# A planner that lays out five engines in time: mended durations, port locks and a third raw buffer

## The chip, the cores and the metric

The kernel runs on one core of a Trainium2 chip. Its engines take instructions each from a queue of their own: TensorE (PE, matmuls and transposes), VectorE (DVE), ScalarE (ACT), GpSimd (POOL) and SyncE (SP, which here only issues DMAs). The metric is the time of one execution on the chip in microseconds, the median of several runs.

## What is computed

Attention with four sink columns and a window of 128, in 4 batches of 8 heads over 768 rows of 64 elements, and behind it two matmuls with h cos h between them, for 3072 tokens:

```python
scores = scale * np.matmul(q, k.transpose(0, 1, 3, 2))
keep = is_sink | in_window            # pos < n_sink, or 0 <= row - pos < window
a = softmax(np.where(keep, scores, -1e9))
x = np.matmul(a, v)                   # (4, 8, 768, 64) -> x (3072, 512)
h = x @ w_in                          # (3072, 512) @ (512, 2048)
g = h * np.cos(h)
return (g @ w_out).astype(np.float32) # (3072, 2048) @ (2048, 512)
```

The weights reach the kernel as 64-bit floats, read as pairs of 32-bit integers.

## The kernel before

The 3072 tokens are 12 chunks of 256. A chunk has 8 slots; in a slot 256 of the 2048 columns of h are made (L419), turned into g on ACT and DVE (r L434 and L441, g L452, glo L464), and multiplied with their rows of w_out into two accumulators (acc, L479; in chunk 0, L474). A product of single precision is three matmuls of the parts hi and lo: xhi·lo_in, xhi·hi_in, xlo·hi_in. Chunk 0 multiplies g by w_out in full precision instead.

The weights come in 32 pieces, 16 of w_in and 16 of w_out, 512 KB each as 64-bit numbers. A piece is loaded into one of two raw buffers (`load`, L532), and DVE makes 32-bit numbers of it in three instructions, a shift (L540) and two passes (top L546, low L552). ACT rounds it to the part hi (L579), and POOL or DVE subtracts that to get lo (L582, the remainder). All of this happens in the first 125 us, while the first three chunks' attention runs.

The 24 early heads (`NEH`, those of the first chunk of three batches) load q and k in natural layout (L817), turn them on PE (`pe_turn` L825), copy them out (L409 on DVE, L407 on ACT; names tq, firsts), make scores (s, L850), mask and take the exponential (p, L919 and on ACT), divide (the norm, L953, on POOL, DVE or ACT), turn p on PE (tp, L1025), copy that (firsts), and multiply by v (av, L1077; the input x is split with L354 and the casts xhi and xlo). Later heads have q and k turned by DVE (L807, L879) after loads at L763 and L776, and split scores (s, L906).

All of that, apart from the setup ahead and the last rows behind, is laid out by `Plan.order`: each step was added with the engines it may run on and their durations, what it depends on, and a due time worked out from the constants in `C`. The planner goes through a time of its own. Whenever an engine is free it takes, of the steps whose dependences are done there, the one with the earliest due time, with penalties for POOL (`POOLPEN`) and for other than the first engine (`ALT`). A step that may use the port that POOL and DVE share is marked `port`; of those, one runs at a time. What comes out is a fixed order of instructions on every engine; on the chip each engine goes through its list and waits where a dependence is not there yet. The 160 idle matmuls (`FILL`, L1379) are steps with the latest due time of all, so PE takes one wherever in the planner's time it has nothing else.

## Time and profile before

| what | us |
|---|---|
| median of 3 runs | 741.33 (741.26 to 741.88) |
| the profiled execution | 741.67 |
| its span | 739.9 |
| busy in the span: PE | 722.6 (98%) |
| DVE | 617.0 (83%) |
| ACT | 551.7 (75%) |
| POOL | 195.7 (26%) |
| DMA of raw pieces, 32 of 512 KB, issue to landing | 4.6 and 4.0 each |

A busy time counts from the start of an instruction to its end; matmuls of PE and instructions of DVE overlap at their ends, so a busy engine may start the next one sooner than the mean duration says. Where the text speaks of the spacing that a form holds, it means start to start when the next instruction follows at once.

### The profile page before, as it was taken

The numbers are of one execution on the slowest core, as the hardware profiler recorded it, in microseconds if no ns is written. First come the engines' busy times: TensorE is split into PE (matmuls) and PEld (weight loads), VectorE is DVE, ScalarE is ACT, GpSimd is POOL, SyncE is SP. The second block draws the span as 40 slices with busy tenths as digits, with TensorE's granted clock in tenths as the row PEclk, the third lists the DMA queues.
The fourth block names the chain that finished last, engine by engine and source line by source line (L and its number), as shares of the span: only waits on it lengthen the run. The fifth ranks groups of instructions, "written<-read, shape, count | busy, mean of one in ns | idle before, by whom it ended". The sixth has DMA issues, their size and how long they took to land.

```text
span 739.9 us, 15112 instructions
## 1 busy us (share of the span) xinstructions
PE 722.6 (98%) x4827; PEld 643.5 (87%) x4827; DVE 617.0 (83%) x1679; ACT 551.7 (75%) x1371; POOL 195.7 (26%) x306
## 2 busy tenths in 40 slices
PE   8989999999999999999999999999999999999996
PEld 8777666799999989998979998989999999999995
DVE  6999999768999899999989988987988998875432
ACT  4979777547878878888878798897789789774322
POOL 2201131001434343244334344333112233231000
PEclk9999999999999999999999999999999999999999
DMA  5765655122555465456565342232233332110000
GB/s 150 200 180 163 185 153 185 54 35 41 146 126 115 104 165 139 91 124 150 153 144 142 89 101 50 58 66 43 47 83 56 56 82 53 22 46 2 30 1 32
DMA packets 215896, 71.48 MB, mean 97 GB/s; under 512 B 204288, under 2 KB 204800, under 8 KB 215808
## 3 DMA queue, kind: packets, MB, share of 16 engines
q1 hardware_dynamic: 215232, 70.17, 39.8%
q8 instruction: 40, 0.66, 0.4%
q14 instruction: 48, 0.39, 0.2%
q10 hardware_dynamic: 576, 0.26, 0.1%
HBM read 64.10 MB, written 6.29 MB: 95 GB/s over the span
## 4 chain that ended last, share of the span: by engine, by line
PE 81%; DVE 10%; DMA 3%; ACT 2%; issue 2%; SPq 1%; DVEq 0%; ACTq 0%
PE h L419 32%; PE acc L479 31%; PE av L1101 5%; PE s L906 4%; PE tp L1021 2%; PE acc L474 2%; DMA raw<-in_moe_w_in_dram 1%; PE av L1077 1%; PE idle L1379 1%; DVE w_out L546 1%; DVE p L919 1%; PE s L850 1%; DVE w_in L546 1%; PE tp L1025 1%; DVE w_in L552 1%
## 5 line engine op out<-in xcount | busy, mean ns | idle before, releaser
L419 PE MATMUL h<-xhi,lo_in 128*128 128x256 f32 x768 | 224.1, 292 | 1.2 <-DVE g L452 0.8
L419 PE MATMUL h<-xlo,hi_in 128*128 128x256 f32 x768 | 216.9, 282 | 0.0
L419 PE MATMUL h<-xhi,hi_in 128*128 128x256 f32 x768 | 216.7, 282 | 0.0
L419 PEld LDWEIGHTS h<-xhi,lo_in 128*128 128x128 f32 x768 | 146.0, 190 | 6.2 <-DVE g L452 2.6
L419 PEld LDWEIGHTS h<-xhi,hi_in 128*128 128x128 f32 x768 | 146.3, 191 | 2.6 <-issue 0.5
L419 PEld LDWEIGHTS h<-xlo,hi_in 128*128 128x128 f32 x768 | 146.2, 190 | 0.0
L479 PE MATMUL acc<-hi_out,ghi 128*128 128x512 f32 x350 | 141.2, 404 | 0.0
L479 PE MATMUL acc<-hi_out,glo 128*128 128x512 f32 x350 | 137.6, 393 | 0.0
L479 PE MATMUL acc<-lo_out,ghi 128*128 128x512 f32 x350 | 137.4, 392 | 0.0
L1060 POOL TENSOR_SCALAR_AFFINE_SELECT pz<-pz 128x512 fp32r<-128x512 f32 x128 | 83.9, 655 | 106.7 <-DVE pz L1047 84.2
L919 DVE CUSTOM_DVE_ANT_0 p<-s,mk 128x264 f32<-128x264 f32 (+1 forms) x192 | 75.2, 399 | 23.2 <-PE s L906 18.6
L928 ACT ACTIVATE p<-p,st 128x264 f32<-128x264 f32 (+1 forms) x192 | 93.6, 490 | 0.5
L428 ACT ACTIVATE yt<-h 128x512 int32<-128x512 f32 x96 | 57.1, 595 | 49.1 <-PE h L419 48.4
L434 DVE SCALAR_TENSOR_TENSOR r<-h,yt 128x512 f32<-128x512 f32 x96 | 65.5, 682 | 30.1 <-ACT yt L428 29.8
L441 ACT ACTIVATE r<-r,neg 128x512 f32<-128x512 f32 x96 | 69.0, 723 | 14.4 <-DVE r L434 13.8
L479 PEld LDWEIGHTS acc<-hi_out,glo 128*128 128x128 f32 x350 | 65.7, 188 | 14.9
L479 PEld LDWEIGHTS acc<-hi_out,ghi 128*128 128x128 f32 x350 | 66.0, 188 | 8.0 <-DVE raw L409 0.4
L479 PEld LDWEIGHTS acc<-lo_out,ghi 128*128 128x128 f32 x350 | 66.0, 189 | 7.7
L464 DVE TENSOR_TENSOR glo<-h,ghi 128x512 fp32r<-128x512 f32 x88 | 59.8, 679 | 9.4 <-ACT ghi L458 8.6
L446 DVE TENSOR_TENSOR h<-h,r 128x512 f32<-128x512 f32 x88 | 60.3, 687 | 5.0 <-ACT r L441 5.0
L458 ACT CAST ghi<-h 128x512 fp32r<-128x512 f32 x88 | 51.1, 581 | 16.9 <-PE acc L479 16.3
L906 PE MATMUL s<-r,l 128*128 128x264 f32 (+2 forms) x288 | 61.0, 293 | 1.3 <-DVE l L873 0.8
(145 smaller groups left out, 1347.6 us busy)
## 6 DMA issues: line engine op xcount, KB each, us to landing
raw<-in_moe_w_in_dram SPq DMA_DIRECT2D x32, 512.0 KB, 4.6
raw<-in_moe_w_out_dram SPq DMA_DIRECT2D x32, 512.0 KB, 4.0
xk<-in_k_dram SPq DMA_DIRECT2D x256, 48.0 KB, 2.0
v<-in_v_dram SPq DMA_DIRECT2D x64, 96.0 KB, 2.2
out_dram<-raw SPq DMA_DIRECT2D x22, 256.0 KB, 2.1
xq<-in_q_dram SPq DMA_DIRECT2D x144, 32.0 KB, 1.8
v<-in_v_dram SPq DMA_DIRECT2D x32, 64.0 KB, 3.9
xq<-in_q_dram SPq DMA_DIRECT2D x24, 64.0 KB, 2.9
```

The source lines that it names most:

```text
L419: nc.tensor.matmul(out=o.h[:, t, :], lhsT=w[:, fs], rhs=xx[:, c, :], start=(c == 0 and n == 0), stop=(c == NC - 1 and n == 2),)
L428: nc.scalar.activation(out=yt, in_=o.h, func=AF.Copy, scale=INV2PI, bias=0.25)
L434: nc.vector.scalar_tensor_tensor(out=o.r, in0=o.h, scalar=INV2PI, in1=yt, op0=ALU.mult, op1=ALU.subtract)
L441: nc.scalar.activation(out=o.r, in_=o.r, func=AF.Sin, scale=TWOPI_DOWN, bias=quarter)
L446: nc.vector.tensor_tensor(out=o.h, in0=o.h, in1=o.r, op=ALU.mult)
L458: nc.scalar.copy(out=o.ghi, in_=o.h)
L464: e.tensor_tensor(out=o.glo, in0=o.h, in1=f32(o.ghi), op=ALU.subtract)
L479: nc.tensor.matmul(out=x.acc[j], lhsT=gg[:, t, j * P : (j + 1) * P], rhs=w, start=(f == 0 and n == 0), stop=(f == NFT - 1 and n == 2), ski ...
L906: nc.tensor.matmul(out=o.s_ps[j][:, :w], lhsT=o.l[:, j * P : (j + 1) * P], rhs=r.rearrange("p n s -> p (n s)")[:, c0 : c0 + w], start=(n = ...
L919: nc.vector.tensor_tensor_reduce(out=o.p[:, j, :w], in0=o.s_ps[j][:, :w], in1=masks[min(o.i0 + j, 2)][:, :w], op0=ALU.add, op1=ALU.min, sc ...
L928: nc.scalar.activation(out=o.p[:, j, :w], in_=o.p[:, j, :w], func=AF.Exp, bias=o.lead.st[:, 0, o.nth, j : j + 1], scale=-1.0, accum_out=o. ...
L1060: nc.gpsimd.affine_select(out=env.pz4[:, :, :, n], in_=f32(env.pz4)[:, :, :, 0], pattern=[[0, 2], [0, CB], [sign, P]], compare_op=ALU.is_g ...
```

## The change

`Plan.order` is written anew, and all constants in `C` are other numbers. Two lines of the table:

```diff
-    "AE": 4.623, "ALT": 3.697, ..., "FILL": 160, ..., "POOLF": 3.143, "POOLPEN": 4.319, ..., "RAW": 2,
+    "AE": 20.521, "ALT": 6.034, ..., "GAP": 0.45, ..., "PASS": 0, ..., "POOLF": 0.749, "POOLPEN": 21.171, ..., "RAW": 3,
```

The planner has tables for what it took as one number: how much of an instruction overlaps with the next (`OVERLAP`), how long after the end of an instruction another engine can start (`LAT`, with `DRAIN` for PE's results and `FETCH` for PE's start), and a model of the DMA queue with a rate (`RATE`, 275 KB per us). Of `port` and the new `lock` steps, a DVE step in `port` waits for a POOL step in `lock` and the reverse, where before every POOL step held the port against both. Rules that kept POOL away from work that DVE would wait for (`NW`, `NWF`, `BLF`) are gone. There may be passes backward in time, but `PASS` is 0. The cores of the new functions, as they stand in the changed kernel:

```python
    OVERLAP = {"PE": 0.0, "ACT": 0.10, "POOL": 0.0, "DVE": 0.08, "SP": 0.0}
    DRAIN = 0.163
    FETCH = 0.06
    RATE = 275.0
    ...
    def place(self, links, prio, begin, on, land, back):
        ...
                for i in ready[e]:
                    if gone[i]:
                        continue
                    if e == "DVE" and i in port and pool_end > now + 1e-9:
                        continue
                    if e == "POOL" and i in lock and dve_end > now + 1e-9:
                        continue
                    key, tab = prio[i], steps[i][4]
                    if tab and tab != table:
                        key += C["PEN"]
                    if not back and len(took[i]) > 1:
                        mine = (took[i][e] - self.OVERLAP[e]) * (C["POOLF"] if e == "POOL" else 1.0)
                        if any(max(free[o] - now, 0.0) + d - self.OVERLAP[o] < mine for o, d in took[i].items() if o != e):
                            continue
                        key += C["POOLPEN"] if e == "POOL" else C["ALT"] * (steps[i][0][0][0] != e)
                    if best is None or (key, i) < best:
                        best = (key, i)
        ...
    def order(self, begin=None, passes=0, filler=None, until=None):
        ...
        start = self.place(links, [s[3] for s in steps], begin, on, land, False)
        for _ in range(passes):
            ...
        if filler is not None:
            t, m = begin["PE"], 0
            for i in sorted((i for i in range(n) if on[i] == "PE" and start[i] <= start[until]), key=lambda i: start[i]):
                while start[i] - t > C["GAP"]:
                    out.append((t, n + m, filler(m), "PE"))
                    t, m = t + 0.13, m + 1
                t = start[i] + held(i)
```

So idle matmuls are no longer steps: one is put every 0.13 us into those planned gaps of PE that are longer than 0.45 us, up to the first acc of chunk 0. There are 84 of them.

Durations of steps and buffers, as far as the text speaks of them:

```diff
-    xq_t = lp.tile([P, 8, 32], F32, name="xq")
-    xk_t = lp.tile([P, 4 * KB, 32], F32, name="xk")
+    xq_ts = [lp.tile([P, 8, 32], F32, name=f"xq{n}") for n in range(2)]
+    xk_ts = [lp.tile([P, 4 * KB, 32], F32, name=f"xk{n}") for n in range(2)]
...
     def dve(n, two=False, ptr=False):
-        return ((n / 2 if two else n) + 62) / 960 + (0.06 if ptr else 0)
+        return ((n / 2 if two else n) + 62) / 960 + (0.145 if ptr else 0.085)
 
     def act(n, sbuf=True):
-        return n / 1200 + (0.092 if sbuf else 0.051)
+        return n / 1200 + (0.192 if sbuf else 0.151)
...
-                        add([("PE", 0.655)], h_mm(o, x, tt, half), d + mm[-1:], t + C["DH"] + (3.5, 5.8)[tt] + 0.6 * half)
+                        add([("PE", 0.735)], h_mm(o, x, tt, half), d + mm[-1:], t + C["DH"] + (3.5, 5.8)[tt] + 0.6 * half)
...
-                bx, btk, b1, b2 = buf("xk", 1), buf("tk", 1), buf("r1", 1), buf("r2", 1)
-                i = add(dma(4), load_k(o), [bx], t - 7 * T + DQ + 1.2, lat=2.4)
+                bx, btk, b1, b2 = buf("xk", 2), buf("tk", 1), buf("r1", 1), buf("r2", 1)
+                o.xk = xk_ts[bx.nth][:, : o.nkb * 4]
+                i = add(dma(2.1), load_k(o), [bx], t - 7 * T + DQ + 1.2, more=307)
...
-        for n in range(int(C["FILL"])):
-            idle.users.append(add([("PE", 0.11)], fill(n), idle.users[:1] or [idle, env.minus], 1e4 + n))
-        env.minus.users += idle.users
...
-        emit(plan.order(BEGIN), setup)
+        emit(plan.order(BEGIN, C["PASS"], fill, xs[0].om[0][0]), setup)
...
-    nc = _bacc.Bacc("TRN2", target_bir_lowering=False, num_devices=1)
+    nc = _bacc.Bacc("TRN2", target_bir_lowering=False, num_devices=1, dynamic_dma_scratch_size=256)
```

The last acc step of a chunk also gets dependences on the ones before it. Line numbers are some 50 higher in the changed kernel (h L473, acc L528 for chunk 0, passes L600 and L606, remainder L636, tp L1078, copies on DVE L463, g L506, idle matmuls L1433).

The order moves as follows. On SP, at the start of the program (raw, xq, xk and v are the tiles loaded; numbers tell buffers apart), before:

```order
L817 DMA xq<-in_q_dram 128x2x64 x2
L817 DMA xk<-in_k_dram 128x2x64 x2
L532 DMA raw_70<-in_moe_w_in_dram 128x1024
L532 DMA raw_71<-in_moe_w_in_dram 128x1024
L798 DMA v_74<-in_v_dram 128x2x64 x2
L747 DMA xb<-in_v_dram 32x1x64 x4
L817 DMA xq<-in_q_dram 128x2x64 x2
L817 DMA xk<-in_k_dram 128x2x64 x2
L817 DMA xq<-in_q_dram 128x2x64 x2
L817 DMA xk<-in_k_dram 128x2x64 x2
L532 DMA raw_70<-in_moe_w_in_dram 128x1024
```

and after:

```order
L870 DMA xq_73<-in_q_dram 128x2x64 x2
L870 DMA xk_75<-in_k_dram 128x2x64 x2
L586 DMA raw_70<-in_moe_w_in_dram 128x1024
L586 DMA raw_71<-in_moe_w_in_dram 128x1024
L586 DMA raw_72<-in_moe_w_in_dram 128x1024
L870 DMA xq_74<-in_q_dram 128x2x64 x2
L870 DMA xq_73<-in_q_dram 128x2x64 x2
L870 DMA xk_76<-in_k_dram 128x2x64 x2
L870 DMA xk_75<-in_k_dram 128x2x64 x2
L851 DMA v_77<-in_v_dram 128x2x64 x2
L802 DMA xb<-in_v_dram 32x1x64 x4
L870 DMA xq_74<-in_q_dram 128x2x64 x2
```

Three raw loads now stand at the front instead of two, and the second pair's xq and xk loads stand ahead of v's.

On PE, at the start (qk is a turned q or k, s a score), before:

```order
L240 MATMUL warm<-ident 128x128 x4
L1379 MATMUL idle<-gt 128x256 x8
L825 MATMUL qk_0_0_144<-ident,xq 128x128 x2
L1379 MATMUL idle<-gt 128x256 x7
L825 MATMUL qk_0_0_144<-ident,xk 128x128 x2
L1379 MATMUL idle<-gt 128x256 x13
L850 MATMUL s_0_0_0_188<-firsts,tq_0_0_154 128x2x128
L850 MATMUL s_0_0_1_192<-firsts,tq_0_0_154 128x512
L1379 MATMUL idle<-gt 128x256 x13
L825 MATMUL qk_0_2_218<-ident,xq 128x128 x2
```

and after:

```order
L294 MATMUL warm<-ident 128x128 x4
L1433 MATMUL idle<-gt 128x256 x2
L878 MATMUL qk_0_0_139<-ident,xq_73 128x128 x2
L1433 MATMUL idle<-gt 128x256 x3
L878 MATMUL qk_0_0_139<-ident,xk_75 128x128 x2
L1433 MATMUL idle<-gt 128x256 x6
L903 MATMUL s_0_0_0_166<-firsts,tq_0_0_146 128x2x128
L903 MATMUL s_0_0_1_175<-firsts,tq_0_0_146 128x512
L1433 MATMUL idle<-gt 128x256 x29
L878 MATMUL qk_0_2_234<-ident,xq_74 128x128 x2
```

The same work stands in the same sequence, with other numbers of idle matmuls between.

On DVE, the last ten instructions up to the one named in the prediction (g of slot 7), before:

```order
L546 SCALAR_TENSOR_TENSOR w_out_1519<-raw_70,w_out_1519 128x512
L552 SCALAR_TENSOR_TENSOR w_out_1519<-raw_70,w_out_1519 128x512
L540 TENSOR_SCALAR w_out_1538<-raw_71 128x512
L546 SCALAR_TENSOR_TENSOR w_out_1538<-raw_71,w_out_1538 128x512
L552 SCALAR_TENSOR_TENSOR w_out_1538<-raw_71,w_out_1538 128x512
L582 TENSOR_TENSOR lo_out_1554<-w_out_1388,hi_out_1432 128x512
L582 TENSOR_TENSOR lo_out_1561<-w_out_1442,hi_out_1489 128x512
L434 SCALAR_TENSOR_TENSOR r_1564<-h_1480,yt 128x512
L582 TENSOR_TENSOR lo_out_1566<-w_out_1452,hi_out_1476 128x512
L452 TENSOR_TENSOR g_1572<-h_1393,r_1478 128x512
```

and after, up to the copy of tp of head 4, which the next tp on PE needs:

```order
L488 SCALAR_TENSOR_TENSOR r_1413<-h_1328,yt 128x512
L606 SCALAR_TENSOR_TENSOR w_out_1405<-raw_71,w_out_1405 128x512
L1006 TENSOR_SCALAR p_0_6_1263<-p_0_6_1263,st_0_4_1105 128x128
L1006 TENSOR_SCALAR p_0_6_1263<-p_0_6_1263,st_0_4_1105 128x256
L594 TENSOR_SCALAR w_out_1425<-raw_72 128x512
L463 COPY firsts<-tp_0_3_1278 128x384
L506 TENSOR_TENSOR g_1431<-h_1283,r_1397 128x512
L600 SCALAR_TENSOR_TENSOR w_out_1425<-raw_72,w_out_1425 128x512
L506 TENSOR_TENSOR g_1440<-h_1328,r_1413 128x512
L463 COPY firsts<-tp_0_4_1446 128x384
```

In the stretch of before stand three remainders lo_out and in that of after none; two norms (L1006) and two copies of tp stand there instead. Those two instructions are the 265th on DVE in both, if the reads of accumulators (which have no row of their own in the count) are left aside.

On PE, the rows ahead of that wait, before, where the last row waits for that g:

```order
L354 MATMUL av_0_2_1494<-xhi_1446,gt 128x512
L1025 MATMUL tp_0_5_1545<-ident,p_0_5_1228 128x128 x3
L474 MATMUL acc_1_955<-w_out_1442,g_1364 128x512
L474 MATMUL acc_0_945<-w_out_1452,g_1364 128x512
L474 MATMUL acc_1_955<-w_out_1452,g_1364 128x512
L1077 MATMUL av_0_4_1568<-firsts,v_74 128x256
L1077 MATMUL av_0_4_1568<-firsts,v_74 128x128
L474 MATMUL acc_0_945<-w_out_1519,g_1468 128x512
L419 MATMUL h_1580<-xhi_793,lo_in_273 128x256
```

and after, where the last row waits for that copy:

```order
L1130 MATMUL av_0_2_1417<-firsts,v_77 128x256
L1130 MATMUL av_0_2_1417<-firsts,v_77 128x128
L1078 MATMUL tp_0_4_1446<-ident,p_0_4_1104 128x128 x3
L473 MATMUL h_1452<-xhi_711,lo_in_277 128x256
L473 MATMUL h_1452<-xhi_711,hi_in_227 128x256
L473 MATMUL h_1452<-xlo_772,hi_in_227 128x256
L473 MATMUL h_1452<-xhi_711,lo_in_294 128x256
L473 MATMUL h_1452<-xhi_711,hi_in_271 128x256
L473 MATMUL h_1452<-xlo_772,hi_in_271 128x256
L408 MATMUL av_0_2_1417<-xhi_1380,gt 128x512
L1078 MATMUL tp_0_5_1463<-ident,p_0_5_1193 128x128 x3
```

The h tile in the rows of before is slot 1 of chunk 1, in those of after an earlier one; both stretches have acc, av, tp and h mixed, at different places of the work.

## Rows read from the trace of the kernel before

**Rows 1.** Table by stretches, one core; columns as its first line says.
```profile
core 0: us, PE busy (x) PEld busy (x) DVE busy (x) ACT busy (x) POOL busy (x), PEclk, DMA share, GB/s
0.00:10.00 10.00, 8.52 (x46) 7.64 (x47) 4.56 (x26) 2.59 (x5) 2.86 (x11) 1.00 0.56 152
10.00:20.00 10.00, 9.49 (x74) 8.70 (x73) 8.58 (x29) 6.74 (x24) 1.30 (x1) 1.00 0.63 172
20.00:61.00 41.00, 38.11 (x245) 31.52 (x244) 37.66 (x117) 34.26 (x99) 5.04 (x5) 1.00 0.65 179
61.00:128.00 67.00, 62.68 (x335) 45.15 (x333) 65.00 (x145) 54.87 (x137) 13.28 (x12) 1.00 0.63 177
128.00:370.00 242.00, 242.00 (x1663) 220.22 (x1663) 214.18 (x585) 185.39 (x452) 77.44 (x123) 1.00 0.47 111
370.00:390.00 20.00, 18.62 (x124) 16.25 (x123) 17.74 (x52) 16.05 (x44) 6.11 (x11) 1.00 0.57 133
390.00:733.70 343.70, 343.22 (x2353) 314.02 (x2351) 268.86 (x729) 251.45 (x614) 89.63 (x144) 1.00 0.26 55
733.70:739.90 6.20, 0.00 (x0) 0.00 (x0) 0.42 (x1) 0.37 (x1) 0.00 (x0) 0.73 0.27 87
```

**Rows 2.** Chain of waits after 61 us, prices on TensorE: start us, us, what.
```profile
86.83 0.86 PE acc L474 x2
...
138.57 2.87 PE h L419 x24
```

**Rows 3.** Waits of TensorE, 61 to 139 us: engine line, releaser, us, times, longest.
```profile
PE s L850 <- DVE st L919: 1.7, 2, 1.4
PE h L419 <- DVE g L452: 0.8, 1, 0.8
```

**Rows 4.** Timeline at 128 us: start us, us, engine line op out<-in [idle before <-releaser].
```profile
127.34 0.68 DVE L452 TENSOR_TENSOR g<-h,r 128x512 f32<-128x512 f32 x1
...
128.07 0.19 PEld L419 LDWEIGHTS h<-xhi,lo_in 128*128 128x128 f32 x1 [0.71 <-DVE g L452]
```

**Rows 5.** Waits of VectorE, 0 to 20 us.
```profile
DVE nw L258 <- DMA nw_i<-in_window_dram: 2.6, 1, 2.6
...
DVE lo_in L582 <- ACT hi_in L579: 1.1, 1, 1.1
```

**Rows 6.** Timeline at 39 us: a remainder on GpSimd beside a pass on VectorE.
```profile
39.18 1.27 POOL L582 TENSOR_TENSOR lo_in<-w_in,hi_in 128x512 fp32r<-128x512 f32 x1 [6.30 <-ACT hi_in L579]
39.23 1.76 DVE L546 SCALAR_TENSOR_TENSOR w_in<-raw,w_in 128x512 int32<-128x512 int32 x1
...
41.03 0.69 DVE L552 SCALAR_TENSOR_TENSOR w_in<-raw,w_in 128x512 int32<-128x512 int32 x1
```

**Rows 7.** Groups by form of VectorE, 0 to 128 us: busy us, mean ns.
```profile
L546 DVE SCALAR_TENSOR_TENSOR w_in<-raw,w_in 128x512 int32<-128x512 int32 x16 | 12.1, 759 | 0.5
L552 DVE SCALAR_TENSOR_TENSOR w_in<-raw,w_in 128x512 int32<-128x512 int32 x16 | 12.0, 752 | 0.3
L546 DVE SCALAR_TENSOR_TENSOR w_out<-raw,w_out 128x512 int32<-128x512 int32 x14 | 11.4, 815 | 0.5
L552 DVE SCALAR_TENSOR_TENSOR w_out<-raw,w_out 128x512 int32<-128x512 int32 x14 | 9.6, 683 | 0.3
```

**Rows 8.** Groups by form of GpSimd, 0 to 150 us.
```profile
L582 POOL TENSOR_TENSOR lo_in<-w_in,hi_in 128x512 fp32r<-128x512 f32 x9 | 11.9, 1325 | 65.6 <-ACT hi_in L579 65.6
L582 POOL TENSOR_TENSOR lo_out<-w_out,hi_out 128x512 fp32r<-128x512 f32 x4 | 5.2, 1290 | 18.1 <-ACT r L441 7.6 <-DVE lo_out L582 6.0 <-ACT hi_out L579 4.5
```

**Rows 9.** Wait of SyncE's queue, 360 to 390 us, and the chain there.
```profile
SPq L776 <- DVE tk L879: 3.5, 1, 3.5
...
370.01 2.62 DMA xk<-in_k_dram
```

**Rows 10.** Timeline of TensorE, 3 to 14 us: idle matmuls.
```profile
3.56 2.08 PE L1379 MATMUL idle<-gt 128*128 128x256 f32 x8
...
6.93 1.79 PE L1379 MATMUL idle<-gt 128*128 128x256 f32 x13
```

More of the change, by code (lines that the diff above doesn't have):

```diff
@@ L88, in order @@
             ds.discard(i)
-            wait[i] += len(ds)
-            for d in ds:
-                after[d].append(i)
-        ready = {e: set() for e in ("PE", "ACT", "POOL", "DVE", "SP")}
-        free = dict(begin or dict.fromkeys(ready, 0.0))
-        events = [(0.0, i) for i in range(n) if not wait[i]]
-        heapq.heapify(events)
-        wake = [t for t in free.values() if t]
+            for d in sorted(ds):
+                after[d].append((i, False))
+                before[i].append((d, False))
@@ new lines, in links @@
+        for row in self.bufs.values():
+            row = [b for b in row if b in taker]
+            for b0, b1 in zip(row, row[1:]):
+                if taker[b0] != taker[b1]:
+                    after[taker[b0]].append((taker[b1], True))
+                    before[taker[b1]].append((taker[b0], True))
+        return after, before
+    def place(self, links, prio, begin, on, land, back):
+        after, before = links
+        steps, port, lock, more = self.steps, self.port, self.lock, self.more
+        n = len(steps)
+        nexts, prevs = (before, after) if back else (after, before)
+        wait, es, start = [len(p) for p in prevs], [0.0] * n, [0.0] * n
+        took = [dict(s[0]) for s in steps]
+        ready = {e: [] for e in self.ENGINES}
+        free = dict.fromkeys(self.ENGINES, 0.0) if back else dict(begin)
+        pool_end = dve_end = -1.0
+        table, server, now, left = "exp" if begin else None, 0.0, 0.0, n
+        todo = [(0.0, i) for i in range(n) if not wait[i]]
+        heapq.heapify(todo)
+        wake = sorted(free.values())
@@ L97, in order @@
         heapq.heapify(wake)
[L98 to L101 removed]
+        gone = [False] * n
+        stale = set(self.ENGINES)
         while left:
[L103 to L108 removed]
+            while todo and todo[0][0] <= now + 1e-9:
+                i = heapq.heappop(todo)[1]
+                for e in (on[i],) if back else took[i]:
+                    ready[e].append(i)
+                    stale.add(e)
+            for e in self.ENGINES:
+                if free[e] > now + 1e-9 or not ready[e]:
@@ L138, in order @@
                 i = best[1]
-                engines, fn, _, _, lat, tab = steps[i]
-                dur = dict(engines)[e]
-                if (e == "POOL" or e == "DVE" and i in self.port):
-                    port_free = now + dur
-                    heapq.heappush(wake, port_free)
-                if tab and tab != table:
-                    dur += self.SWITCH
-                    table = tab
-                for other, _ in engines:
-                    ready[other].discard(i)
-                starts.append((now, len(starts), fn, e))
@@ new lines, in place @@
+                t = now
+                if steps[i][4] and steps[i][4] != table:
+                    t, table = t + self.SWITCH, steps[i][4]
+                start[i], on[i], free[e] = t, e, t + held
+                if e == "DVE" and i in port:
+                    dve_end = t + held
+                if e == "POOL" and i in lock:
+                    pool_end = t + held
+                heapq.heappush(wake, t + held)
+                left -= 1
+                if e == "SP" and not back:
+                    server = max(server, t + held + (2.2 if more[i] >= 512 else 1.7)) + more[i] / self.RATE
+                    land[i] = server - t
@@ L1371, in least_flag @@
             )
-        idle = buf("b0", 1)
         def fill(n):
```

254 lines of the change are left out of this document (128 added, 126 removed), and 13 rows, old and new, of the table C.

## The prediction

> **What bounds the kernel now.** I read the table by stretches first [rows 1]. TensorE (PE) is busy for 722.65 of 739.90 us, which looks like a kernel bound by its matmuls, and from 128 us on it is: the rows from 128 to 733.7 have 603.84 us busy of 605.70. But 160 of those matmuls are idle ones, all before 49 us, and matmul rows overlap, so I added up the useful ones by the spacing that each form holds when the next follows at once: 0.12 us for an h matmul (24 in 2.87), 0.43 for one of chunk 0's acc (2 in 0.86) [rows 2], and so for each form. The sum is 668.8 us for the whole kernel. The same count over PE's order gives 73.2 us of useful work ahead of the matmul at 128.1 us, so 54.9 us of the kernel's loss lies before it.
>
> What holds PE back there is VectorE (DVE). It is busy 65.00 of the 67.00 us from 61 to 128 and 37.66 of 41 before that [rows 1]; PE's waits from 61 to 139 us end at DVE instructions [rows 3], the last long one at 128.07 us, where the first h matmul of chunk 1's second slot waits for g of slot 7 (L452), which ends at 128.02 [rows 4]. So the time is: DVE work up to that g, plus DVE's losses until then, plus PE's work behind it, plus what PE still loses, plus the tail of 6.20 us in which PE has nothing left [rows 1] and 1.77 us outside the span (741.67 less 739.90). DVE executes 265 instructions up to that g; at the spacing that each form holds (0.45 us for the shift L540, 0.61 for each of the passes L546 and L552, 0.60 for a remainder L582, 0.21 and 0.34 for a mask L919 of 128 and 256 columns) that is 106.2 us. 128.1 less 106.2 is 21.9 us lost by DVE. Behind it stand 668.8 less 73.2, 595.6 us of PE work, in 605.6 us: 9.9 lost later. The check: 106.2 + 21.9 + 595.6 + 9.9 + 6.2 + 1.7 = 741.5, against 741.67 of this execution and 741.33, the median of the runs. The two differ by 0.05%, so I forecast from 741.67 and take no correction.
>
> **The order itself.** Nothing computed is removed: PE's useful instructions are the same in kind and number. What changes is which work stands ahead of the place where PE waits last for DVE. I counted, for every wait of PE on DVE in the new order, DVE's work up to it less PE's useful work up to it; the largest such lead sets the end if losses are spread alike. Before it is 33.0 us, at the g above. After it is at the transpose of head 5 of the third chunk (tp_0_5_1463), which needs DVE's copy of head 4's: also 265 instructions there, 106.6 us, but only 69.5 us of PE work ahead (198 h matmuls where there were 216, 2.2 us; one acc, three tp and one pair of av fewer, and two s, 1.6 us). The lead is 37.1 us: **+4.1 us**, by count. The reason is visible in DVE's list: four more copies of tp, four more casts of xlo and four more lo_in are on DVE by then, six lo_out, four norms and one r fewer. Ends of this term: if the losses are no longer concentrated ahead of 128 us, the place that counts may be another one; the next candidates, at 90 to 100 us of PE work, have 32.6 in the new order and 28.1 in the old, which is +4.5, so I keep +4.1 for both ends.
>
> **What DVE loses until there.** Of the 21.9 us, 12.2 are idle (10.00 less 4.56, 10 less 8.58, 41 less 37.66, 67 less 65.00) [rows 1], and the rest is in instructions that last longer than they need.
> Start: DVE waits 2.6 us for the window's number, which no order removes, and 1.1 for the first hi_in [rows 5]. In the new order the shift and both passes of two more pieces stand ahead of that lo_in, so the 1.1 goes; the third raw load is issued at once, where SP before sent it only when the first was used up, and I take 0.6 from the 1.42 idle between 10 and 20 us for it; two copies now stand ahead of the limits, 0.3 later. Sum **-1.4** (ends 0 and -2.5).
> 20 to 61 us: 3.34 idle, mostly single waits for s, tp and xlo. With three raw pieces on the chip DVE more often has a conversion to do meanwhile. Nothing in the trace prices this; it lies between 0 and -3.3, and I take about half, **-1.5**, since the next stretch, where conversions are plenty, shows that such waits shrink to 2.0 in 67.
> 61 to 128 us: of those 2.0 idle I take half, **-1.0**.
> Blocked passes: a pass that runs alone is 0.69 us; the same pass is 1.76 when it starts 0.05 us after a remainder on GpSimd (POOL), and ends 0.54 after that one has ended [rows 6]. By form, the two passes of w_in and the first of w_out average 759, 752 and 815 ns where the second of w_out averages 683 [rows 7]: 16 x 0.076 + 16 x 0.069 + 14 x 0.132 = 4.2 us, beside 13 remainders on POOL that take 17.1 us [rows 8]. The new planner bars such pairs in both directions and gives POOL 11 remainders instead of 13 ahead of the wait, but 15 norms instead of 4, POOL work 26.8 us instead of 23.6. At 4.2/17.1 = 0.25 us per us that is +0.8 if the planner's bars don't hold; -4.2 if they hold throughout. The planner's clock drifts from the chip's, so I take a third, **-1.3**.
>
> The Trainium skill ("SBUF — State Buffer", section "Who interferes with whom") says that a DVE instruction with two SBUF inputs contends with a GpSimd one that reads SBUF, and that the port pair is an exclusive lock. The two rows of the blocked pass agree. By an exclusive lock alone the 3.2 us of added POOL work would cost up to 3.2 us instead of my -1.3, and the sum would be 742.2; it speaks against a change that gives POOL more, and D below is the rival in which it decides.
>
> **What PE loses later.** 1.38 us of PE's idle time lies at 370 to 390 us [rows 1], where the load of xk waits 3.5 us for its only buffer and then takes 2.62 [rows 9]. The second xq and xk buffers remove that: -1.4. Another 3.1 us go, by the count of useful work, between the wait at 128.1 us and a last one at 138.4; I take half of it, -1.5, together **-2.9** (ends 0 and -6). Against it: POOL's whole work rises from 198 to 240 us and norms go there from ACT (81 to 42), so p arrives later at tp. ACT, with 543 us instead of 570, is no bound.
>
> **Fillers.** 160 idle matmuls become 84. They run where PE waits for others: 15 last 1.79 us before an s that waits anyway [rows 10], and PE has 16.6 us of useful work before 49 us. Cost taken: 0. All stretches show a granted clock of 1.00 [rows 1], yet the first eight, at 3.56 us, take 2.08 us where thirteen later take 1.79 [rows 10], so an interval of half speed exists. If the clock were at its lower level (1.2 instead of 2.4 GHz) in the longer gaps, each s, tp and av on the turn between DVE and PE would last 0.1 to 0.4 longer: between 0 and +3 us, hidden while DVE has other passes.
> The tail is not touched: its copies and stores are the same, **0**.
>
> **Sum.** 741.67 + 4.1 - 1.4 - 1.5 - 1.0 - 1.3 - 2.9 = **737.7 us**.
>
> **The rivals.**
> *A, the forecast:* 737.7, by itself 735 to 740. For it: the waits that go have names and rows. Chance 0.40.
> *B, DVE's losses nearly vanish.* If the planner's mended durations keep DVE at 10 us of loss (2.6 for the window's number, 2.8 before anything can arrive, 4.6 elsewhere) and PE at 5 later, 668.8 + 37.1 + 10 + 5 + 6.2 + 1.7 = 729. For it: only 5.4 of 21.9 us are fixed by the start. Against it: a static order meets waits where its times are off by tenths. Chance 0.17.
> *C, the change doesn't do what it says:* plans by durations don't reach the chip's waits, the new order's lead is paid for by what the buffers bring, and the time stays at about 741.7. Chance 0.14.
> *D, slower: DVE's lead turns against the new order.* The lead of +4.1 is counted, the savings are estimates. If DVE loses 21.9 as before, the time is 741.67 + 4.1 less 0 to 2.9, 742.9 to 745.8. On top POOL: behind the wait it has 39 us more than before, at 0.25 us per us 9.6 us of DVE, and DVE's lead in the new order is still 13.1 us at 200 us of PE work (4 before) and reaches zero only at about 300 (240 before), so some 3 us of this would stand on the path: 746 with half of the later savings. It decides from the point where DVE saves less than 4.1 us ahead of the binding wait. Chance 0.29.
>
> **How the numbers follow.** A measurement of this kernel can tell 0.2%, 1.5 us, from no change: 740.2 to 742.8 is the same. A lies below but for 0.05, B below, C inside, D above but for 0.01: faster 0.35 + 0.17 = 0.52, same 0.14 + 0.05 + 0.01 = 0.20, slower 0.28. The range reaches from B's time to D's upper part, 728 to 748, and leaves out less than 2 in 10. Forecast 737.7.
>
> **What would show it.** The lead: PE should last wait for DVE at a tp or an h near 120 to 124 us, with about 69.5 us of useful work done. The start: no wait of lo_in for hi_in of 1 us. Blocking: passes L600 and L606 averaging near 0.70 us (right) or above 0.76 (D). The buffers: 370 to 390 with PE fully busy. Wrong would be: DVE idle for more than 12 us before the last wait, a wait of PE for DVE beyond 200 us, or a granted clock below 1.00 in the first 60 us.

## The result: slower by 0.9%

| | before | after |
|---|---|---|
| median, us | 741.30 (740.97 to 741.88) | 748.30 (746.54 to 749.19) |
| ratio | | 1.0089, 95% interval 1.0072 to 1.0106 |
| the profiled execution, span | 741.67, 739.9 | 749.19, 747.5 |

The table by stretches of the kernel after answers to [rows 1] (same columns; the last two borders follow its longer span):

```profile
0.00:10.00 10.00, 7.45 (x28) 6.31 (x28) 3.89 (x20) 1.85 (x3) 2.87 (x11) 1.00 0.64 185
10.00:20.00 10.00, 8.86 (x63) 7.48 (x62) 9.60 (x34) 6.21 (x19) 1.20 (x1) 1.00 0.52 118
20.00:61.00 41.00, 35.19 (x201) 27.99 (x201) 36.04 (x121) 31.95 (x94) 6.39 (x11) 0.96 0.67 189
61.00:128.00 67.00, 62.31 (x320) 43.74 (x320) 65.76 (x150) 52.14 (x130) 16.66 (x17) 1.00 0.68 180
128.00:370.00 242.00, 238.46 (x1628) 214.69 (x1627) 214.84 (x586) 178.32 (x435) 92.61 (x141) 1.00 0.46 106
370.00:390.00 20.00, 19.35 (x139) 17.30 (x138) 19.39 (x50) 15.18 (x39) 13.84 (x20) 1.00 0.75 202
390.00:743.30 353.30, 350.78 (x2383) 318.02 (x2382) 272.19 (x722) 246.63 (x588) 105.95 (x175) 1.00 0.25 52
743.30:747.50 4.20, 0.00 (x0) 0.00 (x0) 0.42 (x1) 0.37 (x1) 0.00 (x0) 0.92 0.39 131
```

Two things are new. From 128 to 370 us TensorE (PE), which had no idle time there before, is idle for 3.54 us, and from 390 on for 2.52 instead of 0.48. And from 20 to 61 us the granted clock is 0.96.

The waits of PE after 150 us. The names: l is the lo part of q, vr the parts of v, st the sums of the exponential, pz the turned p that POOL masks, gc the sink columns and gp the same turned, glo the lo part of g. Before (engine, line, releaser: us, times, longest):

```profile
PE s L906 <- DVE l L873: 0.8, 1, 0.8
PE s L906 <- DVE st L919: 0.5, 1, 0.5
PE h L419 <- DVE glo L464: 0.3, 1, 0.3
PE tp L1021 <- DVE pz L1047: 0.2, 1, 0.2
```

and after:

```profile
PE tp L1074 <- DVE p L1006: 2.3, 5, 0.8
PE gp L1058 <- DVE gc L1048: 1.4, 3, 0.7
PE tp L1074 <- DVE pz L1100: 1.1, 3, 0.7
PE s L959 <- DVE st L972: 0.7, 2, 0.4
PE av L1154 <- POOL pz L1113: 0.5, 2, 0.3
PE av L1154 <- POOL vr L1019: 0.4, 1, 0.4
```

None is long. There are many of them, all ahead of steps of the late heads' attention: the transposes tp and gp, the scores s and av.

**A better measure than idle time.** Matmul rows overlap, so a PE that starts late often still looks busy. For every profile I added up, record by record, the spacing that each form of matmul holds (0.120 us for h, 0.230 for acc, 0.429 for a record of chunk 0's acc, 0.108 for tp, and so on, the same for all kernels; idle and warm matmuls count nothing). All kernels have 689.4 us of such useful work. The *loss* at some point is the time less the useful work done. Two figures of it tell nearly everything: the **early loss**, at 125 us of useful work (about 160 us of time), and the **late loss**, what is added from 150 us of useful work (about 186 us) to 670.

| us | early loss | late loss |
|---|---|---|
| before | 35.9 | 8.2 |
| after | 35.8 | 17.7 |

So the whole difference arises late: +9.5 us there, -0.1 early and -2.0 in the tail (4.20 us for 6.20) make 7.4 of the 7.5 us between the two profiles. What the change does to the first 140 us, on which most of the prediction is spent, came to nothing in this profile.

### The profile page after: what moved, and what is told of

Same layout as the page of the kernel before. It is cut to its first block, busy times and chain, and to the rows that moved or that the text cites. A ratio compares the mean times of both kernels' runs of the same rounds, so it can differ in the third digit from the quotient of the medians.

```text
span 747.5 us, 14948 instructions
## 1 busy us (share of the span) xinstructions
PE 722.4 (97%) x4751; PEld 635.5 (85%) x4751; DVE 622.1 (83%) x1679; ACT 532.7 (71%) x1304; POOL 239.5 (32%) x373
## 4 chain that ended last, share of the span: by engine, by line
PE 46%; DVE 10%; ACT 9%; issue 3%; POOL 1%; DMA 1%; SPq 0%; DVEq 0%; ACTq 0%; POOLq 0%
PE h L473 19%; PE acc L533 18%; ACT p L981 5%; PE av L1154 4%; PE s L959 3%; DVE p L1006 1%; PE tp L1074 1%; ACT L981 1%; DVE raw L649 1%; DVE h L500 1%; DVE p L972 1%; ACT l L919 1%; DVE l L926 1%; DVE r L488 1%; ACT ghi L512 1%
## 5 line engine op out<-in xcount | busy, mean ns | idle before, releaser
L473 PE MATMUL h<-xhi,lo_in 128*128 128x256 f32 x768 | 223.2, 291 | 0.0
L473 PE MATMUL h<-xlo,hi_in 128*128 128x256 f32 x768 | 217.0, 282 | 0.0
L473 PE MATMUL h<-xhi,hi_in 128*128 128x256 f32 x768 | 216.8, 282 | 0.0
L473 PEld LDWEIGHTS h<-xhi,lo_in 128*128 128x128 f32 x768 | 146.2, 190 | 3.0 <-issue 0.5
L473 PEld LDWEIGHTS h<-xhi,hi_in 128*128 128x128 f32 x768 | 146.2, 190 | 2.9 <-issue 0.7
L473 PEld LDWEIGHTS h<-xlo,hi_in 128*128 128x128 f32 x768 | 146.1, 190 | 0.0
L1113 POOL TENSOR_SCALAR_AFFINE_SELECT pz<-pz 128x512 fp32r<-128x512 f32 x128 | 88.9, 695 | 81.4 <-DVE pz L1100 70.8
L1019 POOL TENSOR_TENSOR vr<-v,vr 128x192 fp32r<-128x192 f32 (+1 forms) x58 | 35.0, 603 | 111.0 <-ACT vr L1014 107.0
```

The source lines that it names most:

```text
L473: nc.tensor.matmul(out=o.h[:, t, :], lhsT=w[:, fs], rhs=xx[:, c, :], start=(c == 0 and n == 0), stop=(c == NC - 1 and n == 2),)
L1019: e.tensor_tensor(out=o.vr[:, :, 1, :], in0=o.v32, in1=f32(o.vr)[:, :, 0, :], op=ALU.subtract)
L1113: nc.gpsimd.affine_select(out=env.pz4[:, :, :, n], in_=f32(env.pz4)[:, :, :, 0], pattern=[[0, 2], [0, CB], [sign, P]], compare_op=ALU.is_g ...
```

## The experiments

Edits to the changed kernel unless another base is named. A median is of 4 to 10 runs, a ratio is against runs of the kernel before on the same chip; early and late loss are those of the one profile of each, and executions of one kernel scatter by 2 to 4 us about their median: the profiles of e9 and e17 are the slowest of their executions, 4 us above the median, that of e10 is the fastest, 3 us below. The late loss of one and the same late order repeats well: after, e6 and e12, which have the same, lost 17.7, 17.6 and 17.5. The last column is worked out from the planner's own table of starts: the time after 150 us in which it leaves PE empty in its own plan.

| run | median | ratio, 95% | early | late | planned gaps |
|---|---|---|---|---|---|
| after | 748.30 | 1.0089 (1.0072 to 1.0106) | 35.8 | 17.7 | 0.0 |
| e1_pe_short | 744.02 | 1.0041 (1.0021 to 1.0062) | 33.7 | 11.2 | 6.4 |
| e2_fetch | 747.76 | 1.0092 (1.0068 to 1.0115) | 33.0 | 15.4 | 1.3 |
| e3_pool_less | 746.30 | 1.0053 (1.0030 to 1.0075) | 36.3 | 12.4 | 0.6 |
| e4_before_pe_long (on before) | 759.99 | 1.0239 (1.0209 to 1.0270) | 38.4 | 26.1 | 2.2 |
| e5_short_less | 752.35 | 1.0148 (1.0111 to 1.0185) | 35.2 | 20.5 | 15.4 |
| e9_slow_others | 748.81 | 1.0094 (1.0058 to 1.0131) | 35.5 | 19.3 | 11.9 |
| e10_slack_less | 746.99 | 1.0103 (1.0066 to 1.0140) | 33.0 | 13.7 | 3.2 |
| e20_low | 747.29 | 1.0095 (1.0066 to 1.0125) | 34.9 | 16.1 | 2.0 |
| e11_slack_all | 741.87 | 1.0021 (0.9997 to 1.0044) | 33.8 | 11.5 | 1.7 |
| e18_slack_attn_low | 746.26 | 1.0062 (1.0044 to 1.0079) | 36.8 | 13.8 | 1.9 |
| e17_slack_attn | 754.54 | 1.0178 (1.0150 to 1.0206) | 37.1 | 22.6 | 11.9 |
| e16_slack_mid | 760.99 | 1.0266 (1.0232 to 1.0300) | 35.0 | 27.7 | 23.2 |
| e14_slack_half | 770.52 | 1.0420 (1.0370 to 1.0470) | 33.9 | 35.5 | 44.3 |
| e15_slack_short | 768.21 | 1.0369 (1.0350 to 1.0387) | 35.8 | 35.6 | 39.7 |
| e6_fills | 749.31 | 1.0107 (1.0084 to 1.0131) | 35.2 | 17.6 | 0.0 |
| e12_v_early | 749.60 | 1.0120 (1.0090 to 1.0150) | 35.0 | 17.5 | 0.0 |
| e13_slack_less_v | 745.19 | 1.0076 (1.0050 to 1.0102) | 35.6 | 11.1 | 1.8 |
| e7_before_bufs (on before) | 754.02 | 1.0169 (1.0143 to 1.0195) | 49.5 | 8.1 | |

### Slack, or POOL: the first four

The theory: the old planner counted 0.655 us for six h matmuls and for three of acc, which take 0.72 and 0.69 on the chip. Its times for PE were 5 to 9% too short, so on the chip the other engines gained on PE all the time. The new planner's 0.735 and 0.71 are 2 to 3% above the chip's, and each attention step stands in PE's order at the moment at which its operand is planned to be ready. The rival: more work on POOL, which blocks VectorE (DVE).

**e1_pe_short**

```diff
-add([("PE", 0.735)], h_mm(...)
+add([("PE", 0.735 if a < 2 else 0.655)], h_mm(...)
-add([("PE", 0.87 if x.full else 0.71)], mm, ...
+add([("PE", 0.87 if x.full else 0.71 if a < 2 else 0.655)], mm, ...
```

> The changed kernel with one thing undone: from chunk 2 on the planner counts 0.655 us for an h step and an acc step on TensorE again, as before, in place of 0.735 and 0.71. In the order this moves nothing before about 150 us. Theory S (slack): up to 140 us both kernels lost the same on TensorE (36.1 us against the sum of its useful matmuls); from there the old one loses 8 us and the new one 18, because the planner's clock for TensorE is now true, so that each tp, s, gp and av of a late head stands in TensorE's order at the very moment at which its operands are planned to be ready, and every delay on the chip is a wait of TensorE. With the short durations the planner thinks TensorE is faster than it is, so on the chip the other engines gain on it: expected 738 to 742 us, with the late loss at 8 to 10 us. Theory P (POOL): the late loss comes from 40 us more work on POOL, which blocks VectorE's instructions at the shared port; POOL's share stays here, so 747 to 749 us.

**e2_fetch**

```diff
-lag += self.FETCH
+lag += self.FETCH + (0.5 if t > 150.0 else 0.0)
```

> The changed kernel, but after 150 us of planner's time an operand that another engine makes for TensorE counts as ready 0.5 us later than before. Theory S: waits of TensorE for tp, s, gp and av after 150 us were 0.3 to 0.9 us each; half a microsecond of planned slack takes most of them: 741 to 744 us. Theory P: no change, 747 to 750 us.

**e3_pool_less**

```diff
+if e == "POOL" and now > 150.0 and steps[i][1].__qualname__.split(".")[-3] in ("norm", "k_lo", "x_lo"):
+    continue
```

> The changed kernel, but after 150 us of planner's time POOL may not take the norm of p, the lo part of k nor the lo part of x, which go to VectorE or ScalarE; POOL's late work falls from 204 to 146 us by the planner's durations, VectorE's rises from 516 to 545. Theory P: VectorE is blocked less (its norms of 128x136 took 442 ns in the changed kernel and 297 before) and TensorE's late loss goes back to 8 to 10 us: 739 to 743 us. Theory S: the slack stays as thin and VectorE has more to do: 747 to 751 us.

**e4_before_pe_long**, on the kernel before

```diff
-add([("PE", 0.655)], h_mm(...)
+add([("PE", 0.735 if a > 1 else 0.655)], h_mm(...)
-add([("PE", 0.858 if x.full else 0.655)], mm, ...
+add([("PE", 0.858 if x.full else 0.71 if a > 1 else 0.655)], mm, ...
```

> The kernel before with only the planner's durations of TensorE's two main steps made long from chunk 2 on, 0.735 for an h step and 0.71 for an acc step instead of 0.655. Theory S: this alone takes the old order's hidden slack away: 744 to 749 us, with a late loss of 12 to 18 us. Theory P: POOL's work stays near 155 us, so 740 to 742 us, the same as before.

Measured: both theories hold a part. The short durations took 6.5 us of late loss out of the changed kernel (4.3 us by the medians), and the long ones put 17.9 into the old one, nearly twice the most that the theory gave. The waits of PE in e1 after 150 us are these; none of tp and gp is left, and what shows is the way from glo back to an h buffer:

```profile
PE h L473 <- DVE glo L518: 2.8, 3, 1.2
PE av L1154 <- POOL pz L1113: 0.8, 1, 0.8
PE s L959 <- DVE l L926: 0.3, 1, 0.3
```

How thin the slack is can be read from the traces with the planner's own dependences: of 127 late transposes (L1074), 5 started within 0.15 us of the end of their last operand before, 24 after, 4 in e1 and 20 in e4. It is the thin ones that count, not the middle: the median slack was 1.10, 0.74, 1.16 and 2.49 us. In e4 POOL is busy for 182 us between 150 and 735 us, where before it was 172 and after 211, and the norm on DVE takes 310 ns; so POOL has little part in what e4 lost. One thing stays open there: the constants in `C`, which set the due times, were the old kernel's, and whether others would suit the long durations no run tells.

e3 took 5.3 us of late loss out by the rival's way, though only 2.0 us by the medians, and its interval just touches that of after. The norm of 128x136 on DVE, from 150 to 600 us, before, after and in e3 (busy us, mean ns):

```profile
L953 DVE TENSOR_SCALAR p<-p,st 128x136 f32<-128x136 f32 x33 | 8.2, 297 | 0.1
```

```profile
L1006 DVE TENSOR_SCALAR p<-p,st 128x136 f32<-128x136 f32 x42 | 16.4, 442 | 0.3
```

```profile
L1008 DVE TENSOR_SCALAR p<-p,st 128x136 f32<-128x136 f32 x59 | 15.3, 302 | 0.3
```

With fewer steps on POOL the norm is back at its old duration, so POOL had blocked it by 0.14 us in the mean. The mean hides the ones that matter: of the 42, 17 take less than 0.29 us, and five that start 0.05 us behind POOL's lo part of k (L950) take 1.10 to 1.12. One of the five, the transpose that waits for it as the last line (three norms are merged in the first):

```profile
317.75 1.74 DVE L1006 TENSOR_SCALAR p<-p,st 128x136 f32<-128x136 f32 x3
317.99 1.06 POOL L950 TENSOR_TENSOR r<-tk,r 128x408 fp32r<-128x408 f32 x1
...
319.28 0.30 PE L1074 MATMUL tp<-ident,p 128*128 128x128 f32 x1 [0.76 <-DVE p L1006]
```

The five waits of PE for the norm on DVE, the first line of the waits of after, 2.3 us in all, are these five. So the two causes are links of one chain there: the planner had barred the pair, on the chip it met all the same, and the transpose behind it had too little room for the 0.8 us. The Trainium skill ("SBUF — State Buffer", "Who interferes with whom") counts tensor_scalar among the DVE instructions that can enter a mode with both port pairs, when their operands allow it, and says that whichever of DVE and GpSimd issues first then blocks the other fully; these rows agree.

e2 fell between: the expected small waits went (9 of 127 transposes within 0.15 us), but three waits for POOL's selection, up to 1.6 us, and one of 1.5 for ScalarE came in their place. Its median, 747.76, is no gain.

### Does the sum of both, or more of one, give more?

**e5_short_less** is e1 and e3 together, **e10_slack_less** e2 and e3.

> The changed kernel with both edits of the first group that helped: the planner's short durations of TensorE from chunk 2 on and, after 150 us, no norm, lo part of k nor lo part of x on POOL. Counted from 150 us of useful TensorE work to the end, TensorE lost 17.7 us in the changed kernel, 11.2 with the short durations, 12.4 with less on POOL, 8.2 before. If the two causes are separate (slack, and blocking by POOL), they add: 6 to 9 us, 739 to 743. If both edits only give VectorE's and POOL's work a better place in the same way, the sum stops at 10 to 12: 742 to 745.

> The changed kernel with half a microsecond of planned slack ahead of TensorE after 150 us and, from there on, no norm, lo part of k nor lo part of x on POOL. With the slack alone the small waits of tp and gp went, and what was left were a few longer waits for POOL's selection (pz, up to 1.6 us) and for ScalarE's norm: a late loss of 15.4 us. With POOL's work alone cut it was 12.4. If the two are links of one chain (p arrives late at TensorE either by TensorE's thin slack or since POOL is late), both together bring 8 to 10 us, 739 to 743 us. If POOL's part and the slack are exchanged for waits elsewhere each time, 12 to 16 us, 744 to 748.

**e9_slow_others**

```diff
+slow = 1.09 if now > 150.0 and e in ("ACT", "DVE", "POOL") else 1.0
-held = took[i][e] - self.OVERLAP[e]
+held = took[i][e] * slow - self.OVERLAP[e]
```

(and the same factor in the two lines that set a lag).

> The changed kernel, but after 150 us the planner counts 9% more time for every step of VectorE, ScalarE and POOL, with TensorE's true durations. Theory S2 (ratio): what the old order had was that TensorE was planned 5 to 9% faster than the chip against the other engines; if only that ratio counts, this order does as the one with the short durations: late loss near 11 us, 742 to 745 us. If it is the short durations themselves that matter (which order the due times give when TensorE is not the planned bound), the others' longer ones make it worse or leave it: 747 to 752 us.

**e11_slack_all**; **e20_low**, **e16_slack_mid** and **e14_slack_half** have 0.15, 0.35 and 0.5 instead of 0.25; **e15_slack_short** is e11 and e1 together.

```diff
-lag = took[a][ea] + (...) + self.LAT.get((ea, eb), 0.03)
+lag = took[a][ea] + (...) + self.LAT.get((ea, eb), 0.03) + (0.25 if t > 150.0 else 0.0)
```

> The changed kernel, but after 150 us the planner adds 0.25 us to every step's way from one engine to another, not only ahead of TensorE. If the late loss is the missing slack of the whole chain of s, mask, exponential, norm, tp, copy, selection and av, this one takes most of it: late loss 9 to 12 us, 740 to 744. If not, 746 to 749 as with the slack ahead of TensorE.

> The changed kernel with 0.15 us on every way between engines after 150 us, the low side of the dose: late loss between 11.5 (0.25 us) and 17.7 (0), 13 to 16 us, 743 to 746.

> The changed kernel with 0.35 us on every way between engines after 150 us: a point between 0.25 and 0.5. Slack as the cause: a late loss of 8 to 11 us, 738 to 742 us, between the neighbours.

> The changed kernel with 0.5 us more planned on every way between engines after 150 us, twice the amount that brought the late loss from 17.7 to 11.5 us. If the loss is missing slack it falls on, to 8 to 10 us: 738 to 741. If the planner is by then so slow in its own time that its order runs TensorE's work too early and attention too late for the buffers, the loss rises: 745 us or more.

> The changed kernel with both edits that gave slack: 0.25 us on every way between engines, and the planner's short durations of TensorE from chunk 2 on. Each alone left a late loss of 11.5 and 11.2 us. If both give the same thing, slack against TensorE, together they bring 8 to 10 us, and with 34 us of early loss 737 to 741 us. If what is left at 11 us is something else, 741 to 744.

Measured: 0.25 us on every way brought the late loss to 11.5 and the time to that of the kernel before (1.0021, interval 0.9997 to 1.0044), as the slack theory has it; 0.15 gave 16.1, in its place between. But 0.35 and 0.5 gave 27.7 and 35.5, and each pair of helpful edits was no better than its parts or much worse (13.7, 20.5, 35.6). Of these five doses 0.25 is the best. Whether that is the dose or the one order that came of it, the runs don't tell: each edit lays out another order (after and e11 have a third of PE's steps in the same place), and e13 below, which has e10's two edits and one load moved at the start, lost 11.1 late where e10 lost 13.7. Nor is e11 slack alone: its norms on DVE are 22 at 298 ns instead of 42 at 442. The largest waits of PE in e16 after 150 us say where the excess is:

```profile
PE h L473 <- DVE glo L518: 7.7, 8, 2.0
PE tp L1074 <- DVE p L1006: 2.0, 1, 2.0
PE gp L1058 <- DVE gc L1048: 1.7, 2, 0.9
```

A part of the excess is the clock. In five of the six runs with planned gaps of 11.9 us or more (all but e17) the granted clock fell after 150 us, in e16 to 0.81 in this stretch (columns as in [rows 1]) and once more at 480 to 488:

```profile
352.00:360.00 8.00, 5.99 (x30) 5.02 (x29) 6.69 (x24) 7.88 (x23) 3.61 (x8) 0.81 0.23 39
```

In no other run did it. By the shares of the clock that are missing, an estimate, it is 1.7 us of PE's work in e9, 3.4 in e5, 3.5 in e16 and 5 in e14 and e15. Without it e9 and e5 would have lost 17.6 and 17.1, as the changed kernel; the rest of e16, e14 and e15 is far above that.

e9, which should have done as e1 if only the ratio of planned speeds counted, gained nothing, by its median of 748.81 either. By the ratio alone the gain of e1 can't be explained.

### Where the excess comes from

**e17_slack_attn** and **e18_slack_attn_low** give 0.35 and 0.25 us only to ways out of attention's steps:

```diff
+DENSE = ("h_mm", "turns", "rest", "cosine", "gate", "g_hi", "g_lo", "out_mm", "out_end", "out_copy")
-... + self.LAT.get((ea, eb), 0.03)
+... + self.LAT.get((ea, eb), 0.03) + (0.35 if t > 150.0 and steps[a][1].__qualname__.split(".")[-3] not in DENSE else 0.0)
```

> The changed kernel with 0.35 us more planned after 150 us on every way out of a step of attention, but none out of the steps of the dense part (h, yt, r, g, ghi, glo, acc). With 0.35 us on all ways the late loss was 27.7 us and TensorE's largest waits were those of h for glo, 7.7 us, which the changed kernel does not have. Theory T (trade): the dense loop from h to glo and back to an h buffer got as much planned latency as attention and fell behind; spared that, the loss is 9 to 13 us, 740 to 745. Rival L (length): any slack that makes the plan itself longer than TensorE's work loses what it gains, since the planner lets TensorE wait in its own time and orders by that: 18 to 28 us, 749 to 760.

> The same with 0.25 us. Theory T: as with 0.25 us on all ways (late loss 11.5) or a little better, 9 to 12 us, 739 to 742. Rival L: the plan is hardly longer than with 0.25 us on all ways, so 740 to 743 too.

Sparing the dense loop saved 5.1 us of the late loss (22.6 for 27.7; 6.5 by the medians), not 15 to 19, and at 0.25 us it was no help (13.8 for 11.5). The length of the plan orders the runs better. Within the new planner, all with planned gaps of 3.2 us or less lost 11 to 18, those with 11.9 to 23.2 lost 19 to 28, the two with about 40 lost 35.5; e1, with 6.4 gaps and 11.2, stands apart, since its planned PE is faster than the chip's. Of e16's 23.2 us of planned gaps 13.4 stand ahead of h steps, where PE's largest waits on the chip are. The reading that fits: a planner that leaves PE empty in its own time lays the work out by that pace, and a fixed order doesn't catch up on the chip, so slack that the plan pays with gaps is lost again. No run varies the gaps alone, so this is argued from the order of the runs, not shown.

### The first 60 us

**e6_fills**

```diff
+if "values_pe" in steps[i][1].__qualname__ and not held_av:
+    held_av = True
+    for _ in range(14):
+        out.append((start[i] - 1e-6, n + m, filler(m), "PE"))
+        m += 1
```

> The changed kernel with 14 idle matmuls more, right ahead of the first av, where TensorE waited 1.9 us for the load of v, its granted clock fell to 0.66 of the stretch from 30 to 35 us and VectorE idled 2.5 us there. Theory C (clock): the idle matmuls bridge the wait, the clock stays at 1.00 and the loss at 20 us of useful work is 25 to 26 us instead of 27.8: 745 to 747 us. Rival: VectorE paces TensorE there anyway and 14 matmuls of 0.12 us only come on top: 748 to 750.

**e12_v_early** (and **e13_slack_less_v**: this edit, e2's and e3's)

```diff
-o.vl = add(dma(1.0), load_v_pair(...), o.bxs, t - 2 * T + DV + 3.2, more=128)
+o.vl = add(dma(1.0), load_v_pair(...), o.bxs, t - 2 * T + DV + 3.2 if g else -999.0, more=128)
```

> The changed kernel with one load moved: the first v load stands on SyncE's queue right behind the three raw loads, ahead of the second pair's q and k. In the changed kernel TensorE waited 1.9 us for it at 26 to 28 us, the clock fell to 0.66 of the stretch from 30 to 35 us, and the loss at 20 us of useful work was 27.8 us; in profiles with the same early order whose clock stayed at 1.00 it was 25.0 and 25.6. If that wait brings the clock down, it is gone: loss 25 to 26, 745 to 747 us. If the stall only moves to the q and k loads behind it, 748 to 750.

> The changed kernel with the three edits that the last three runs make apart: slack ahead of TensorE and less on POOL after 150 us, and the first v load earlier. If each does what its run is to show, early loss 33.5 us, late loss 9 and the tail as before: 736 to 740 us, faster than the kernel before. If one of them fails, 741 to 746.

The stretch from 20 to 40 us of the kernel after, in fives (columns as in [rows 1]), then the same of e11, which has the same order there:

```profile
25.00:30.00 5.00, 2.53 (x14) 1.61 (x13) 4.12 (x17) 4.84 (x17) 2.40 (x4) 1.00 0.65 169
30.00:35.00 5.00, 5.00 (x23) 4.25 (x22) 2.52 (x10) 2.08 (x10) 0.05 (x1) 0.66 0.66 177
```

```profile
25.00:30.00 5.00, 4.44 (x26) 3.25 (x25) 4.93 (x21) 4.51 (x16) 2.09 (x4) 1.00 0.71 175
30.00:35.00 5.00, 4.74 (x27) 3.27 (x26) 4.10 (x18) 4.80 (x17) 1.56 (x3) 1.00 0.75 204
```

In the first, PE waits 1.9 us for v, is busy for half of the stretch, and in the next one the granted clock is 0.66, part of it at the lower of its two levels (1.2 and 2.4 GHz). One order, two outcomes: of 14 profiles with this early order, nine have the dip, with a mean early loss of 35.8 us, and five have not, with 33.5. So the dip goes with 2.3 us, of which the missing third of the clock over five microseconds is 1.7, and without it the new order's early part is 2.4 us better than the old one's 35.9. The wait for v alone doesn't decide it: e14 waited 1.8 us and has no dip, e16 waited 1.2, e20 had no such wait, and both have the dip.

The two edits didn't win that back. e6 kept the clock at 1.00, but the 14 idle matmuls (1.7 us) came on top: 35.2. e12 removed the wait and the dip, and PE waited for firsts and for a norm on POOL instead: 35.0. That the edits kept the dip away is not shown by one profile of each, since five of 14 had none anyway. e13 ended at 745.19, as its weaker expectation has it, with a late loss of 11.1, no better than e11's.

**e7_before_bufs**, on the kernel before:

```diff
-"RAW": 2
+"RAW": 3
-xq_t = lp.tile(...)
+xq_ts = [lp.tile(...) for n in range(2)]
...
```

(xk and the rings in the same way).

> The kernel before with the buffers of the changed one and nothing else: three raw buffers, two for xq and two for xk, its own planner and constants. If the buffers pay by themselves, the load of xk at 370 us no longer waits (1.4 us of TensorE there), and VectorE idles less between 20 and 61 us: 737 to 740 us. If the old order does not profit since its due times send the loads when they were sent anyway: 740 to 743 us.

Measured: 13 us slower, all of it early (49.5; late 8.1 as before). The third raw load now stands ahead of the second pair's q and k, but so it does in the changed kernel, whose loads at the start are the same but for one place; so the place of the load can't be all of it. Three stretches of e7:

```profile
15.00:20.00 5.00, 5.00 (x31) 4.42 (x30) 3.65 (x10) 3.53 (x13) 1.27 (x1) 0.82 0.18 38
50.00:55.00 5.00, 2.36 (x8) 1.29 (x8) 4.54 (x16) 4.93 (x15) 0.00 (x0) 0.93 0.87 260
55.00:61.00 6.00, 5.28 (x17) 4.03 (x17) 4.08 (x10) 2.68 (x7) 1.76 (x1) 0.50 0.50 156
```

The clock falls twice, and PE waits 2.7 us once for xq. A buffer was no gain by itself under the old constants; which step of the old order loses by it stays open. The wait of 370 us [rows 9] went, as expected, but the late loss stayed at 8.1: what it freed was lost elsewhere.

No run beat the kernel before; the best, e11, equals it.

## Why the prediction was wrong, point by point

**The order's lead, +4.1.** Right in sense. The count had an error: a full-precision matmul is two records in the trace, so a row of chunk 0's acc costs 0.86 us, not the 0.43 that I read off one record, and the useful work is 689.4 us, not 668.8. Recounted, the lead goes from 14.0 to 18.6 us, +4.6. The same error made up the 3.1 us that I saw lost between 128 and 138 us: PE has no idle time there [rows 1], and the -1.5 taken for it had no ground.

**DVE's losses ahead of the wait, -5.2.** Right as a sum, not in its parts: at the wait named, where tp starts at 123.8 us, the same count gives 17.2 us for 21.9, -4.7. But DVE's idle time to 128 us rose from 12.2 to 12.7 (6.11, 0.40, 4.96 and 1.24 by the table above): the wait of lo_in went, and so did that for the window's number, which I had called fixed, but a copy of tq that now stands first waits 3.6 us for PE; from 20 to 61 us, where I took -1.5, the wait for v and the dip made +1.6. All of the gain is in instructions that were stretched. The passes of the conversions after, as in [rows 7]:

```profile
L600 DVE SCALAR_TENSOR_TENSOR w_in<-raw,w_in 128x512 int32<-128x512 int32 x16 | 11.7, 738 | 0.1
L606 DVE SCALAR_TENSOR_TENSOR w_out<-raw,w_out 128x512 int32<-128x512 int32 x16 | 11.7, 733 | 0.0
L600 DVE SCALAR_TENSOR_TENSOR w_out<-raw,w_out 128x512 int32<-128x512 int32 x16 | 10.9, 681 | 0.1
L606 DVE SCALAR_TENSOR_TENSOR w_in<-raw,w_in 128x512 int32<-128x512 int32 x16 | 10.8, 681 | 0.1
```

16 x 0.057 and 16 x 0.052 above 681 ns are 1.7 us, where it was 4.2: the new locks work for the passes, -2.5 for my -1.3. Counted from start to start instead, the passes' excess over their spacing fell from 6.2 to 2.5 us and that of the shifts from 2.9 to 1.5, which is about the whole of the gain.

Lead and savings cancelled, -0.1 for my -1.1, and the early loss is 35.8 for 35.9.

**The fillers, 0, with 0 to +3 as bound.** The upper part of the bound, if the missing idle matmuls are the reason, which no run shows: 2.3 us where the clock dips, in nine of 14 profiles; they stand within the sums above. (The row read as "15 last 1.79 us" has thirteen matmuls.) I had taken it that DVE hides it; DVE itself idles for 2.48 of the five microseconds at the lower clock.

**What PE loses later, -2.9: the step that failed.** It came to +9.5. The named wait at 370 to 390 us did shrink, from 1.38 to 0.65 us of idle time. What I did not see is that the old order's quiet stretch after 140 us rested on durations that the change mends: 0.655 for 0.735 us is in the diff, and I read it as an improvement of the plan. I looked for where the plan waits and not for how much room it leaves. e4 shows this slack as a cause by itself, e1 and e11 agree; that POOL's blocking is another is shown by the five norms of 1.1 us with PE's waits behind them, and its size, by e3, is 5.3 us of late loss or 2.0 by the medians. I had it in rival D, at 3 us. About 3 us between e1 or e11 and the kernel before (11.2 to 11.5 against 8.2) I can't assign.

**The tail, 0.** 4.20 us here for 6.20 [rows 1], but e6, with the same end, has 5.9 us: from PE's last work to the end of the span it is 4.2 or 4.3 us in two profiles and 5.8 to 7.0 in the others.

**The rivals.** It ended on D's side, slower, by thin slack behind the wait and POOL, at 748.3 us; D's 746 and the range's 748.0 were too low by what the slack costs. All three signs of being wrong came true: waits of PE for DVE beyond 200 us, DVE idle for more than 12 us ahead of the last early wait, and a granted clock of 0.96 from 20 to 61 us.

## What to carry to other kernels

A fixed order needs room for what the plan doesn't know. A plan whose bottleneck is counted too long or too short isn't wrong in the same way: the one here that counted the bound engine 5 to 9% too short gave the other engines slack, and mending that number alone made the old order 2.4% slower. When durations are mended, put the slack back on purpose, try several small doses, and be wary where the plan itself begins to leave the bound engine empty. Judge a new order by two counts together: how many of the bound engine's instructions start right when their operand ends (5 before, 24 after), and how long the plan leaves that engine empty. Neither is enough alone: e16 has only 9 of the former and lost 27.7 us, and after has no planned gap at all.

## What was not expected of the hardware

One and the same early order ran with and without a dip of the granted clock to 0.66 in one 5 us stretch, and 2.3 us apart in the mean. The length of TensorE's longest wait ahead of it doesn't tell the two apart: the dip came behind waits of 1.9 us (after) and 1.1 us (e20), and stayed away behind 1.8 (e14). A norm on VectorE that started 0.05 us behind a subtraction on GpSimd took 1.10 to 1.12 us instead of 0.28. A full-precision matmul of 512 columns stands in the trace as two records of 0.43 us each.
